# p times v in plain float32 with p summed beside it, and inputs laid out by the host, in a pooled attention with a feed-forward part

## The chip, the cores and the metric

The kernel runs on one core of a Trainium2 chip. The metric is device microseconds from start to end of one execution. Five engines have their own instruction streams, in order: TensorE (PE; its weight loads are listed apart as PEld), VectorE (DVE), ScalarE (ACT), GpSimd (POOL) and SyncE (SP), which here only issues DMAs.

## The reference

```
q, k, v: (8, 8, 1152, 64) float32; w_in (512, 2048), w_out (2048, 512)
q_pool = mean of neighbouring pairs of queries           # 576 queries of a head
scores = q_pool @ k.T / 8;  scores -= max over the keys
p = exp(scores);  p /= sum(p) + 1e-9
x = (p @ v), heads side by side                          # (4608, 512)
h = x @ w_in;  out = (h - tanh(h)) @ w_out               # (4608, 512)
```

The weights come as float64, which the kernel turns into float32 itself, from integer words.

## The kernel before, in words

Most products run on operands of type float32r (F32R), a float32 with a short mantissa. Every float32 is split into hi = f32r(x) and lo = f32r(x - hi), and a product of two of them is made of three: hi\*hi, hi\*lo and lo\*hi.

**Attention.** Heads are taken in 32 pairs (two heads fill 128 feature rows). A pair has `U` = 36 score units: two halves of the queries (288 each, `HQ`), three groups of three key tiles in each half, two heads, three key tiles. One `score_unit` is two products into a PSUM tile `ps_s` (`t1`: hi\*lo + lo\*hi by 128 contraction rows; `t2`: hi\*hi and minus the maximum by 66 rows) and an exponential on ScalarE, into `p_f`. Keys are on the partitions, queries run along the free axis.

*p times v* (`split_p`, `pv_slot`). ScalarE rounds three key tiles of exponentials to `p_h`; GpSimd (two in three) or VectorE (one in three) subtracts to get `p_l` in bfloat16. A 128-column operand `v_w` holds hi and lo of a head's v and a column of ones, so that one float32r product per key tile, head and half gives p_h times both parts of v and the sum of p. What is left (p_l times hi of v, p_l times one, p_h times the left-out column) are six bfloat16 products for each key tile, 32 or 64 columns wide, which are placed side by side on the array (`tile_position`). `v_part` prepares `v_w` on GpSimd.

*Maximum* (`max_part`, `max_rows`). For each pair, 27 products of 384 keys into `ps_m` (three buffers) and a VectorE `tensor_reduce` of each. Twenty-four of them contract over 64 rows only (one head), the three others over 128 rows with a block operand `bd`. `max_rows` takes the results through DRAM (`m_dram`) to two rows of `t2`.

*Preparation.* q and k are loaded with the tokens on the partitions; VectorE adds neighbouring queries (`query_sums`), TensorE transposes them (`transposes`), ScalarE and VectorE take hi and lo out of PSUM, and ten DMAs for a pair bring these to where the products need them (`operands`).

*Weights* (`w_block`). 64 blocks of 128x256 float64 words, each some eight VectorE operations and two of GpSimd, spread between the score units.

**Order.** In the attention part every engine keeps the order of the program (`InOrder`). The program goes through the 1152 units; a table (`units`, `rows`, `parts`) says how many units before its first score each step of a pair's preparation is issued, and `add(u, ...)` puts a task beside unit u. So an instruction that waits holds up everything behind it on its engine. DMAs are all issued by SP, in that same order.

**Feed-forward.** Ten chunks of columns: eight of 512 tokens and two of 256. For each there are 16 steps `fc`: `hidden` makes 12 products of 512 columns (hi and lo of x and w_in, `ps_h`), four ScalarE functions, seven VectorE operations and one of GpSimd give h - tanh(h) (the polynomial is used where u = h\*h is below a threshold, `copy_predicated` by a mask `g_m` takes the other value), then ScalarE and GpSimd split it (`g_hi`, `g_lo`). Two steps later (`LAG`) `second` makes 12 products with w_out. `load_x` brings the next chunk's x: for each of four feature tiles, DMAs (`fetch`), then an addition of the lo part on VectorE (L119) and three GpSimd operations (`work`, L120 to L122). Its staging tiles are single (`xt`), so a fetch follows the work before it. In this part a scheduler sets the order.

Of the kernel before, what the change touches and what calls it, by code (L numbers as in the profile page):

```python
# [10 lines left out]
BF16 = mybir.dt.bfloat16  # L11
# [7 lines left out]
# h - tanh(h) = PL * h * u * (u - P0) * ((u + A1)^2 + P1) * ((u + A2)^2 + P2), u = h^2,  # L19
# to float32 precision where |h| < T_POLY; h - tanh(h) itself cancels there  # L20
# [7 lines left out]
class InOrder:  # L28
    """An engine whose instructions keep the order they are written in."""
# [15 lines left out]
def kernel(  # L45
# [33 lines left out]
    pc = const.tile([P, 2], F32, name="pc")  # L79
    nc.vector.memset(pc[:, 0:1], A1)  # L80
    nc.vector.memset(pc[:, 1:2], A2)
    keep = const.tile([P, 1], F32, name="keep")      # 0 where x's lo rows hold the sums
    nc.vector.tensor_tensor(keep, ident[:, 63:64], ident[:, 64:65], op=ALU.add)
    nc.vector.tensor_scalar(keep, keep, -1.0, 1.0, op0=ALU.mult, op1=ALU.add)
# [3 lines left out]
    x_dram = dram.tile([NP, 2, P, NTOK], F32, name="x_dram")  # L88
# [5 lines left out]
    def load_x(tiles, sp, dve, pool, t0, n):  # L94
        """Columns of x, divided by the sums of their softmax, in two parts; in steps."""
# [4 lines left out]
        def fetch(hp):  # L100
            x = xt.tile([P, 512], F32, name="x_f")
            r = xt.tile([P, 512], F32, name="x_r")
            y = xt.tile([P, 512], F32, name="x_g")
            t[hp] = x, y, r
            rows = x_dram[hp].rearrange("h (u p) t -> (h u) p t", u=2)
            sp.dma_start(x[:, 0:n], rows[0:4:3, :, t0:t0 + n])
            sp.dma_start(y[:, 0:n], rows[1:3, :, t0:t0 + n])
# [9 lines left out]
        def work(hp):  # L117
            x, y, r = t[hp]
            dve.scalar_tensor_tensor(x[:, 0:n], y[:, 0:n], keep, x[:, 0:n], op0=ALU.mult, op1=ALU.add)  # L119
            pool.tensor_tensor(x[:, 0:n], x[:, 0:n], r[:, 0:n], op=ALU.mult)  # L120
            pool.tensor_scalar(x_h[:, hp, 0:n], x[:, 0:n], 1.0, 0.0, op0=ALU.mult, op1=ALU.add)  # L121
            pool.tensor_tensor(x_l[:, hp, 0:n], x[:, 0:n], x_h[:, hp, 0:n].bitcast(F32), op=ALU.subtract)  # L122
# [16 lines left out]
    with ExitStack() as actx:  # L139
        # what is free before the end comes last  # L140
# [15 lines left out]
        U = 4 * KT                  # score units of a pair: (half, three key tiles, head, key tile)  # L156
# [4 lines left out]
        tt = [[o.tile([P, 2, KQ], F32R, name=f"t{j}_{i}") for j in (1, 2)] for i, o in enumerate((op0, op))]  # L161
# [15 lines left out]
        nc.gpsimd.memset(one, 0.0)
# [509 lines left out]
```

## Time and profile before

| | |
|---|---|
| median of 3 runs | 2471.56 us (2467.0 to 2481.7) |
| the profiled execution: span | 2467.1 us; the lowest timed run has 2467.0 |
| first score product | at 27.5 us |
| attention ends, feed-forward begins | at 1493 us |
| PE, DVE, ACT, POOL busy over the span | 93%, 78%, 53%, 50% |
| mean granted TensorE clock | 0.88 |

A busy PE includes the time that a matmul's results take to come out, so it is not a PE at its peak; how far apart two products start says more. "L38" (L37 in the changed kernel) stands for all instructions of the attention part, since the helper class records them; they are told apart by the names of their tiles (`out<-in`). An idle time is put down to what ended it.

### The profile page before, as it was taken

How to read it: one execution, taken by the hardware profiler on the slowest of the kernel's cores; microseconds unless marked ns; L12 is line 12 of the kernel's file. 1: busy time of each engine (PE TensorE's matmuls, PEld its weight loads, DVE VectorE, ACT ScalarE, POOL GpSimd, SP SyncE). 2: the span in 40 equal slices, each digit the busy share in tenths (PEclk: the TensorE clock that was granted, in tenths of full speed). 3: DMA queues.
4: the chain of work that ended last, by engine and by line, in shares of the span. 5: the costliest groups of instructions: out<-in, count | busy, mean ns of one | idle time of the engine just before them, and what ended most of it. 6: DMA issues, size and time to landing. Idle time of an engine off the chain costs nothing. (4 is left out here: it accounts for less than half of the span.)

```text
span 2467.1 us, 34314 instructions
## 1 busy us (share of the span) xinstructions
PE 2289.9 (93%) x11921; PEld 1617.4 (66%) x11921; DVE 1926.3 (78%) x3119; ACT 1307.6 (53%) x2663; POOL 1241.7 (50%) x1022
## 2 busy tenths in 40 slices
PE   8999999999999999999999989779798897989988
PEld 5666666666666666666666667557676676767777
DVE  5687887977885868777867978678778786877988
ACT  2555665655664655655645665334444453444545
POOL 3455555555563545555645644554454544444443
PEclk9988887978895878978966979889999999999999
DMA  7355474564654744644644656120110202011010
GB/s 173 91 138 151 109 170 124 140 158 104 153 146 100 170 123 108 164 126 122 181 104 109 142 165 250 53 72 20 52 44 26 59 10 69 15 44 39 5 33 18
DMA packets 202180, 251.67 MB, mean 102 GB/s; under 512 B 92688, under 2 KB 131232, under 8 KB 202008
## 3 DMA queue, kind: packets, MB, share of 16 engines
q1 hardware_dynamic: 202008, 249.49, 38.6%
q8 instruction: 94, 1.54, 0.3%
q14 instruction: 78, 0.64, 0.1%
HBM read 118.93 MB, written 45.56 MB: 67 GB/s over the span
## 5 line engine op out<-in xcount | busy, mean ns | idle before, releaser
L38 POOL TENSOR_TENSOR p_l<-p_f,p_h 128x864 bf16<-128x864 f32 x256 | 531.2, 2078 | 655.9 <-ACT p_h L38 484.5
L38 ACT ACTIVATE p_f<-ps_s 128x288 f32<-128x288 f32 x1152 | 463.1, 412 | 573.0 <-PE ps_s L38 564.2
L38 DVE TENSOR_REDUCE mx<-ps_m 128x1 f32<-128x384 f32 x864 | 453.3, 550 | 295.7 <-PE ps_m L38 290.8
L38 PE MATMUL ps_s<-t 128*128 128x288 f32 (+1 forms) x2319 | 644.3, 368 | 9.1 <-DMA t<-m_dram 8.5
L38 PEld LDWEIGHTS ps_s<-t 128*128 128x128 f32 (+1 forms) x2319 | 429.9, 226 | 114.0 <-issue 23.8
L602 PE MATMUL ps_o<-wo,g_hi 128*128 128x512 f32 x1008 | 295.3, 416 | 70.7 <-ACT g_hi L594 70.7
L38 ACT ACTIVATE p_h<-p_f 128x864 fp32r<-128x864 f32 x384 | 353.0, 919 | 0.0
L575 PE MATMUL ps_h<-x,wi 128*128 128x512 f32 (+1 forms) x1440 | 334.9, 376 | 0.0
L595 POOL TENSOR_TENSOR g_lo<-g_s,g_hi 128x512 fp32r<-128x512 f32 (+1 forms) x160 | 202.3, 1265 | 258.1 <-ACT g_hi L594 186.9
L38 PE MATMUL ps_m<-x 64*128 64x384 f32 x768 | 304.5, 505 | 21.9 <-DVE mx L38 20.6
L38 PE MATMUL ps_o<-p_h,v_w 128*128 128x288 f32 x1152 | 312.9, 369 | 0.0
L575 PEld LDWEIGHTS ps_h<-x,wi 128*128 128x128 f32 x1440 | 262.6, 193 | 54.9
L602 PEld LDWEIGHTS ps_o<-wo,g_hi 128*128 128x128 f32 x1008 | 197.7, 200 | 125.0 <-ACT g_hi L594 83.5
L594 ACT ACTIVATE g_hi<-g_s 128x512 fp32r<-128x512 f32 (+1 forms) x160 | 94.2, 589 | 331.5 <-DVE g_s L593 326.8
L38 PEld LDWEIGHTS ps_o<-p_h,v_w 128*128 128x128 f32 x1152 | 219.6, 231 | 49.0 <-issue 48.5
L38 PEld LDWEIGHTS ps_m<-x 64*128 64x128 f32 x768 | 128.8, 211 | 143.3 <-issue 75.3
L38 PE MATMUL ps_o<-p_l,v_w 128*64 128x288 bf16 x1152 | 198.4, 341 | 0.0
L38 PE MATMUL ps_o<-p_h,v_x 128*32 128x288 bf16 x1152 | 190.9, 328 | 0.0
L38 PE MATMUL ps_o<-p_l,one 128*32 128x288 bf16 x1152 | 188.6, 323 | 0.1
L602 PE MATMUL ps_o<-wo,g_lo 128*128 128x512 f32 x504 | 165.5, 409 | 17.9 <-POOL g_lo L595 17.7
L38 DVE TENSOR_TENSOR p_l<-p_f,p_h 128x864 bf16<-128x864 f32 x128 | 170.3, 1331 | 3.1 <-ACT p_h L38 3.0
L38 DVE TENSOR_SCALAR w<-w 128x256 int32<-128x256 int32 (+1 forms) x192 | 165.9, 864 | 0.2
(82 smaller groups left out, 3171.3 us busy)
## 6 DMA issues: line engine op xcount, KB each, us to landing
t<-x SPq DMA_DIRECT2D x64, 432.0 KB
k_n<-in_k_dram SPq DMA_DIRECT2D x64, 288.0 KB
t<-kq_l SPq DMA_DIRECT2D x64, 288.0 KB
t<-x SPq DMA_DIRECT2D x64, 288.0 KB
v_n<-in_v_dram SPq DMA_DIRECT2D x32, 576.0 KB
x_dram<-o_s SPq DMA_DIRECT2D x32, 576.0 KB
q_n<-in_q_dram SPq DMA_DIRECT2D x32, 512.0 KB
t<-kq_l SPq DMA_DIRECT2D x64, 144.0 KB
```

The lines of the kernel that those rows point to most:

```text
L38: ins = self.tc.keep_in_program_order(f(*args, **kwargs))
L575: nc.tensor.matmul(h, wi[fc][:, w, c], x[:, c, 0:n], start=(j == 0), stop=(j == len(mm) - 1))
L594: nc.scalar.activation(g_h, s1, AF.Copy)
L595: nc.gpsimd.tensor_tensor(g_l, s1, g_h.bitcast(F32), op=ALU.subtract)
L602: nc.tensor.matmul(po[j], g[:, ts], wo[fc][:, w], start=(fc == 0 and i == 0), stop=(fc == NF - 1 and i == 2))
```

## The change

- **p times v.** `split_p`, `pv_slot` and `v_part` go. v is loaded by the host's layout and used as it is: for each key tile, half and head one product of plain float32 operands (`F32`, not `F32R`), v (64 columns) against the exponentials; the first head on array columns 0 to 63, the second on 64 to 127 (`pv`). All six of a group come in one burst.
- **Sums of p.** `z_part` adds the three key tiles of a group: GpSimd with two additions (groups 0 and 2 of a half), VectorE with one `tensor_reduce` over a strided view (group 1). For each half `z_sums` adds over the partitions with six plain float32 products by a block of ones, 32 columns wide, into `ps_z`. They go to DRAM by themselves (`z_dram`).
- **Layouts.** The host orders q, k and v so that the features are on the partitions; transposes go. The query sum is one addition of 128x576, on GpSimd (on VectorE for the first two pairs); hi and lo are taken from SBUF in two pieces. `kq_l` now has one buffer instead of two.
- **Maximum.** All 27 products contract over 128 rows, by a block operand of 128x1152 (`bd`) for each parity, that four DMAs of `max_queries` fill. `ps_m` has two buffers instead of three, `ps_s` four instead of three.
- **Weights.** 32 blocks of 128x512 instead of 64 of 128x256. The first 15 units' extra product goes.
- **Feed-forward.** L119 goes, and so does one of the two big DMAs of a fetch. The mask is made by ScalarE (Relu of u minus the threshold, read as integers). GpSimd's `s2` goes; its constant is added in a VectorE operation. VectorE has six operations instead of seven. The first chunk's `work` is on GpSimd instead of VectorE, and later. Output rows are contiguous.

The diff, cut to its core:

```diff
-            sp.dma_start(x[:, 0:n], rows[0:4:3, :, t0:t0 + n])
-            sp.dma_start(y[:, 0:n], rows[1:3, :, t0:t0 + n])
+            sp.dma_start(x[:, 0:n], x_dram[hp, :, t0:t0 + n])
...
-            dve.scalar_tensor_tensor(x[:, 0:n], y[:, 0:n], keep, x[:, 0:n], op0=ALU.mult, op1=ALU.add)
...
-        ps_m = actx.enter_context(tc.tile_pool(name="ps_m", bufs=3, space=PSUM))
-        ps_s = actx.enter_context(tc.tile_pool(name="ps_s", bufs=3, space=PSUM))
+        ps_m = actx.enter_context(tc.tile_pool(name="ps_m", bufs=2, space=PSUM))
+        ps_s = actx.enter_context(tc.tile_pool(name="ps_s", bufs=4, space=PSUM))
...
+        def max_queries(pi):
+            w = pairs[pi]
+            for h in range(2):
+                r = slice(h * 64, h * 64 + 64)
+                raw_copy(bd[w.i][r, h * 512:(h + 1) * 512], w.hi[r, 0:512])
+                raw_copy(bd[w.i][r, 8 * P + h * 64:8 * P + (h + 1) * 64], w.hi[r, 512:SQ])
...
-            pe.matmul(ps[:, 0:CH], st, mv, start=True, stop=True)
+            pe.matmul(ps[:, 0:CH], bd[w.i][:, t * P:(t + 1) * P], w.hi[:, cs], start=True, stop=True)
...
+        def z_part(grp):
+            z = grp.z = zp.tile([P, 2, HQ], F32, name="z")
+            if grp.g == 1:
+                dve.tensor_reduce(z, grp.p.rearrange("p h j q -> p h q j"), axis=AX.X, op=ALU.add)
+            else:
+                pool.tensor_tensor(z, grp.p[:, :, 0], grp.p[:, :, 1], op=ALU.add)
+                pool.tensor_tensor(z, z, grp.p[:, :, 2], op=ALU.add)
+        def pv(u, grp):
...
+            for j in range(3):
+                kt = 3 * grp.g + j
+                for h in range(2):
+                    pe.matmul(hf.o[64 * h:64 * h + 64, 0:HQ], w.v[:, h, kt], grp.p[:, h, j], start=(kt == 0),
+                              stop=(kt == KT - 1), tile_position=(0, 64 * h))
...
+        def z_sums(u, w, hf):
+            ps = ps_o.tile([P, 512], F32, name="ps_z")
+            for g in range(3):
+                for h in range(2):
+                    r = 64 * (g % 2) + 32 * h
+                    pe.matmul(ps[r:r + 32, 0:HQ], ones, hf.zs[g][:, h], start=(g < 2), stop=(g > 0),
+                              tile_position=(0, r))
...
-            units = dict(load=-93, load_k=-76, query_sums=-82, transposes=-69, last_queries=-53, operands=-36, load_v=-33,
-                         v_part=-18)
+            units = dict(load=-82, query_sums=-68, hi_q=-66, hi_k=-65, max_queries=-64, lo_q=-62, lo_k=-61, operands=-34, load_v=-20)
...
-        nc.gpsimd.tensor_scalar(s2, s2, 1.0, P2, op0=ALU.mult, op1=ALU.add)
+        nc.scalar.activation(m, u, AF.Relu, bias=pc[:, 2:3])
...
-        nc.vector.scalar_tensor_tensor(s1, s1, P1, s2, op0=ALU.add, op1=ALU.mult)
-        nc.vector.tensor_tensor(s1, s1, w, op=ALU.mult)
-        nc.vector.tensor_scalar(m, u, T_POLY * T_POLY, None, op0=ALU.is_ge)
-        last = nc.vector.copy_predicated(s1, m, th).ins
+        nc.vector.scalar_tensor_tensor(w, s2, P2, w, op0=ALU.add, op1=ALU.mult)
+        nc.vector.scalar_tensor_tensor(s1, s1, P1, w, op0=ALU.add, op1=ALU.mult)
+        last = nc.vector.copy_predicated(s1, m.bitcast(I32), th).ins
```

Where instructions stand now. TensorE in the middle of the attention part, before: one key tile's bfloat16 products (v_x, one and v_w are their operands) between two score units and a product for the maximum (ps_m).

```order
L38 MATMUL ps_m_5271<-x_4595 128x384
L38 LDWEIGHTS v_x0_128
L38 MATMUL ps_o0_5226<-p_h_5073,v_x0_128 32x288
L38 LDWEIGHTS v_x0_128
L38 MATMUL ps_o1_5227<-p_h_5123,v_x0_128 32x288
L38 LDWEIGHTS one_130
L38 MATMUL ps_o0_5226<-p_l_5074,one_130 32x288
L38 LDWEIGHTS one_130
L38 MATMUL ps_o1_5227<-p_l_5124,one_130 32x288
L38 LDWEIGHTS v_w01_125
L38 MATMUL ps_o1_5227<-p_l_5124,v_w01_125 64x288
```

The same engine in the middle of the attention part now, where a group's p times v stands between score units.

```order
L37 MATMUL ps_s_10227<-t1_0_121 128x288
L37 MATMUL ps_s_10227<-t2_0_122 128x288
L37 MATMUL ps_o_10178<-p_f_10114,v_9850 64x288 x6
L37 MATMUL ps_s_10238<-t1_0_121 128x288
L37 MATMUL ps_s_10238<-t2_0_122 128x288
L37 MATMUL ps_m_10242<-x_10097,bd0_125 128x384
L37 MATMUL ps_s_10248<-t1_0_121 128x288
L37 MATMUL ps_s_10248<-t2_0_122 128x288
```

The column-tiled products, which came in three short visits for a group, now come in one of six. VectorE, before, in the middle of the attention part: reductions for the maximum between weight steps (w), lo parts (kq_l) and subtractions for p_l.

```order
L38 TENSOR_TENSOR p_l<-p_f,p_h 128x864
L38 TENSOR_SCALAR w_9629<-w_9628 128x256
L38 TENSOR_TENSOR kq_l<-ps_m,x 128x512
L38 SCALAR_TENSOR_TENSOR w_9630<-w_raw,w_9629 128x256
L38 TENSOR_REDUCE mx<-ps_m 128x1 x5
```

VectorE now, at a like place, with a lo part that waits for the DMAs out of the one `kq_l` buffer, and a reduction of p (z).

```order
L37 TENSOR_REDUCE mx<-ps_m 128x1 x5
L37 TENSOR_TENSOR kq_l<-kq,x 128x576
L37 TENSOR_REDUCE mx<-ps_m 128x1
L37 TENSOR_TENSOR kq_l<-kq,x 128x1152
L37 TENSOR_SCALAR w_hl<-w_6599 128x512
L37 TENSOR_REDUCE mx<-ps_m 128x1
L37 TENSOR_REDUCE z<-p_f 128x576
```

The maxima that follow a lo part or a z stand behind it; p_l is gone from this engine.

More of the change, by code (lines that the diff above doesn't have):

```diff
@@ L78 @@
     nc.vector.tensor_copy(ident_r, ident)
-    pc = const.tile([P, 2], F32, name="pc")
+    pc = const.tile([P, 3], F32, name="pc")
     nc.vector.memset(pc[:, 0:1], A1)
     nc.vector.memset(pc[:, 1:2], A2)
[L82 to L88, printed above, removed]
+    nc.vector.memset(pc[:, 2:3], -T_POLY * T_POLY)
+    ones = const.tile([P, 32], F32, name="ones")
+    nc.vector.memset(ones, 1.0)
+    x_dram = dram.tile([NP, P, NTOK], F32, name="x_dram")
+    z_dram = dram.tile([B, 2, 2, NP, SQ], F32, name="z_dram")
     r_dram = dram.tile([B, 2, NP, SQ], F32, name="r_dram")
@@ L102, in fetch @@
             r = xt.tile([P, 512], F32, name="x_r")
-            y = xt.tile([P, 512], F32, name="x_g")
-            t[hp] = x, y, r
-            rows = x_dram[hp].rearrange("h (u p) t -> (h u) p t", u=2)
-            sp.dma_start(x[:, 0:n], rows[0:4:3, :, t0:t0 + n])
-            sp.dma_start(y[:, 0:n], rows[1:3, :, t0:t0 + n])
+            t[hp] = x, r
+            sp.dma_start(x[:, 0:n], x_dram[hp, :, t0:t0 + n])
             c = t0
@@ L231, in query_sums, with hi_part @@
             w.mx = sm.tile([P, 9, 3], F32, name="mx")
             w.hi = x_tile(0)[:, 0:KQ]
-            w.lo = tr.tile([P, KQ], F32R, name="kq_l")
-        def transposes(u, pi, g):
+            w.lo = ld.tile([P, KQ], F32R, name="kq_l")
+        def hi_part(pi, c0, c1):
             w = pairs[pi]
-            blocks = [(w.q_s[:, t], P) for t in range(4)] if g == 0 else []
-            blocks += [(w.q_s[0:64, 4], 64)] if g == 1 else []
-            blocks += [(w.k_n[:, c], P) for c in ((), range(0, 3), range(3, 7), range(7, KT))[g]]
-            ps = ps_m.tile([P, 512], F32, name="ps_m")
-            n = 0
-            for src, m in blocks:
-                pe.transpose(ps[:, n:n + m], src.rearrange("p h d -> p (h d)"), ident[0:m, 0:m])
-                n += m
-            c0 = (0, 512, SQ + 3 * P, SQ + 7 * P)[g]
-            cs = slice(c0, c0 + n)
-            add(u + 1, lambda: act.activation(w.hi[:, cs], ps[:, 0:n], AF.Copy), at=first)
-            add(u + 3, lambda: dve.tensor_tensor(w.lo[:, cs], ps[:, 0:n], w.hi[:, cs].bitcast(F32), op=ALU.subtract))
@@ L376, in pv_out @@
-        def pv_out(u, w, o, half):
-            if half == 0:
-                w.o_s = sm.tile([P, 2, SQ], F32, name="o_s", bufs=1)
-            for h in range(2):
-                act.activation(w.o_s[:, h, half * HQ:(half + 1) * HQ], o[h][:, 0:HQ], AF.Copy)
-            if half == 1:
-                c0 = w.b * SQ
-                add(u + 2, lambda: sp.dma_start(x_dram[w.hp, :, :, c0:c0 + SQ].rearrange("h p t -> p h t"), w.o_s))
+            pass
+        def z_part(grp):
[5 more added lines that the diff above has]
+                pool.tensor_tensor(z, z, grp.p[:, :, 2], op=ALU.add)
@@ new lines, in pv @@
+        def pv(u, grp):
+            w, hf = grp.w, grp.half
+            if grp.g == 0:
+                hf.o = ps_o.tile([P, 512], F32, name="ps_o")
+                hf.zs = []
+            for j in range(3):
[3 more added lines that the diff above has]
+                              stop=(kt == KT - 1), tile_position=(0, 64 * h))
+            hf.zs.append(grp.z)
+            if grp.g == 2:
+                add(u + 1, o_out, w, hf, at=first)
+                add(u + G - 1, z_sums, u + G - 1, w, hf)
@@ new lines, in z_out, with store @@
+        def z_out(u, w, hf, ps):
+            act.activation(w.z_s[:, hf.n * HQ:(hf.n + 1) * HQ], ps[:, 0:HQ], AF.Copy)
+            if hf.n == 1:
+                def store():
+                    sp.dma_start(x_dram[w.hp, :, w.b * SQ:(w.b + 1) * SQ], w.o_s)
+                    for r in range(4):
+                        sp.dma_start(z_dram[w.b, r // 2, r % 2, w.hp:w.hp + 1], w.z_s[32 * r:32 * r + 1])
+                add(u + 2, store)
+                if w.hp == NP - 1:
+                    add(u + 6, lambda: tot.append((w.b, sums(w.b))))
+                    if w.b < B - 1:
+                        add(u + 12, lambda: reciprocals(dve, *tot[0]))
+                        add(u + 15, lambda: spread(sp, *tot.pop(0)))
@@ L386, in sums @@
         def sums(b):
             n = NP * 2 * SQ // P
[L389 to L392 removed]
+            t = rec.tile([P, 2, n], F32, name="rec")
+            for r in range(2):
+                for h in range(2):
+                    sp.dma_start(t[h * 64:h * 64 + 64, r], z_dram[b, r, h].rearrange("a (x n) -> (a x) n", n=n))
@@ L449 @@
             for r in range(f // P, (f + WB) // P):
-                for c in range(0, DM, WB):
-                    blocks.append((1, r, c))
+                blocks.append((1, r, 0))
         for i, blk in enumerate(blocks):
-            u = U + 18 * i - 3 * max(i - 47, 0)
+            u = U // 2 + 34 * i
             add(u, w_block, u, *blk)
@@ L511 @@
             add(u + units["load_v"], load_v, pi)
-            for h in range(2):
-                add(u + units["v_part"] + 18 * h, v_part, pi, h)
             for x, ta, tb in rows:
```

267 lines of the change are left out of this document (88 added, 179 removed).

## The prediction

> **What bounds the kernel now.** I began with the clock, since the page's mean of 0.88 hides two states. Two stretches of the attention part, all engines (us, then busy time and count of PE, PEld, DVE, ACT, POOL, granted clock, DMA share, GB/s):
>
> ```profile
> 280.00:350.00 70.00, 67.97 (x465) 44.34 (x465) 62.80 (x106) 48.22 (x106) 42.07 (x31) 1.00 0.49 132
> 750.00:802.00 52.00, 52.00 (x219) 33.17 (x219) 25.81 (x56) 22.56 (x48) 17.77 (x15) 0.50 0.36 93
> ```
>
> The same two stretches for the score tile `ps_s` alone (PE, PEld, ACT); ACT's count is the number of score units:
>
> ```profile
> 280.00:350.00 70.00, 31.48 (x132) 20.11 (x132) 26.06 (x67) 1.00 0.49 132
> 750.00:802.00 52.00, 22.91 (x60) 15.70 (x61) 12.30 (x30) 0.50 0.36 93
> ```
>
> At full clock a unit takes 70/67 = 1.045 us, a pair of 36 units 37.6 us; at half clock 52/30 = 1.73 us, a pair 62.4. At full clock VectorE is busy for 62.80/70 = 0.90 and TensorE for 0.97: both are nearly used up. At half clock TensorE alone is.
>
> The whole part has its ends in the rows of the first scores and of the first feed-forward product:
>
> ```profile
> L38 PE MATMUL ps_s<-t x2319: 288/300/611, 27.5 to 1482.5; 66*128 66x288 f32 x190, 128*128 128x288 f32 x4
> ```
>
> ```profile
> 1493.03 6.64 PE L575 MATMUL ps_h<-x,t 128*128 128x512 f32 x28
> ```
>
> So it takes 1493 - 27.5 = 1465 us, 45.8 for each of 32 pairs: a mixture of the two states. The feed-forward part has the other 974 us.
>
> What TensorE pays for a product is how far the starts are apart (start, us, form, count), first at full clock, then at half:
>
> ```profile
> 821.14 0.55 PE L38 MATMUL ps_m<-ident,k_n 128*128 128x128 f32 x3
> 821.45 0.51 PE L38 MATMUL ps_o<-p_h,v_w 128*128 128x288 f32 x2
> 821.79 0.43 PE L38 MATMUL ps_s<-t 128*128 128x288 f32 x2
> 822.07 0.34 PE L38 MATMUL ps_m<-x,bd 128*128 128x384 f32 x1
> 822.24 0.43 PE L38 MATMUL ps_o<-p_h,v_w 128*128 128x288 f32 x2
> 822.51 0.43 PE L38 MATMUL ps_s<-t 128*128 128x288 f32 x2
> ...
> 823.40 0.31 PE L38 MATMUL ps_o<-p_h,v_x 128*32 128x288 bf16 x2
> 823.40 0.30 PE L38 MATMUL ps_o<-p_l,one 128*32 128x288 bf16 x2
> 823.63 0.32 PE L38 MATMUL ps_o<-p_l,v_w 128*64 128x288 bf16 x2
> 823.88 0.54 PE L38 MATMUL ps_s<-t 128*128 128x288 f32 x2
> ```
>
> ```profile
> 761.14 0.92 PE L38 MATMUL ps_o<-p_h,v_w 128*128 128x288 f32 x3
> 761.86 0.68 PE L38 MATMUL ps_s<-t 128*128 128x288 f32 x2
> ```
>
> Two float32r products of 288 columns take 0.27 us (822.24 to 822.51), so 0.135 each; 384 columns take 0.17. Four narrow products start together and cost 0.23, not 0.135: going from one tiling of the array to another costs some 0.1. At half clock three products take 0.72, 0.24 each.
>
> **The change part by part: TensorE in the attention.** For a pair: scores 72 x 0.135 = 9.7. Maximum, now 27 products on 128 rows, 27 x 0.17 = 4.6, without the changes of tiling around the 64-row ones. Transposes go. p times v: 18 key tiles (9, two halves), two heads side by side. No row shows a plain float32 product. Its price lies between one float32r pass (0.135) and four (0.54). The nearest row is the transposes of float32 tiles: three of 128 columns in 0.31 us, 0.23 for 288. I take 0.54, above it: the kernel's own splitting shows that the array's operand holds half of a float32, and a whole product of two split numbers is four part products (the kernel before keeps three). 18 x 0.54 = 9.7. Sums of p: two visits of four and two tiles, 4 x 0.54 = 2.2. Eight visits to column tiles, two changes each: 1.6. Transposed maxima: 0.2, an estimate. Together 28.0 us at full clock; at the transposes' price it would be 21.2. At half clock it is (9.7 + 9.7 + 2.2) x 0.24/0.135 + 4.6 x 2 + 1.8 = 49.4.
>
> The Trainium skill ("FP8 and Floating Point Precision", TensorE Precision Notes) has true float32 at four passes; the sum by it is the 28.0. No run here shows it yet.
>
> **VectorE in the attention** decides, I think. Its rows (busy us, mean ns):
>
> ```profile
> L38 DVE TENSOR_REDUCE mx<-ps_m 128x1 f32<-128x384 f32 x864 | 453.3, 550 | 295.7 <-PE ps_m L38 290.8
> L38 DVE TENSOR_TENSOR kq_l<-ps_m,x 128x512 fp32r<-128x512 f32 x64 | 43.7, 683 | 18.9 <-ACT x L38 18.9
> L38 DVE CAST m<-nm 128x10 fp32r<-128x10 f32 x30 | 13.7, 458 | 1.0
> L38 DVE TENSOR_SCALAR w<-w 128x256 int32<-128x256 int32 (+1 forms) x192 | 165.9, 864 | 0.2
> L38 DVE TENSOR_SCALAR w<-w_raw 128x256 int32<-128x256 int32 x128 | 93.2, 728 | 0.0
> L38 DVE SCALAR_TENSOR_TENSOR w<-w_raw,w 128x256 f32<-128x256 uint16 x64 | 62.0, 969 | 0.2
> L38 DVE SCALAR_TENSOR_TENSOR w<-w,w 128x256 int32<-128x256 int32 x64 | 34.4, 538 | 0.8
> L38 DVE TENSOR_SCALAR w_hl<-w 128x256 fp32r<-128x256 f32 x64 | 23.3, 364 | 4.4 <-POOL w L38 4.4
> ```
>
> and, for what 512 columns cost when nothing is in the way (min/median/max ns):
>
> ```profile
> L38 DVE TENSOR_TENSOR x_f<-x_f,x_r x4: 691/692/694, 1433.8 to 1473.6; 128x512 f32<-128x512 f32 x4
> L38 DVE TENSOR_SCALAR x<-x_f x4: 426/428/428, 1434.5 to 1474.3; 128x512 fp32r<-128x512 f32 x4
> ```
>
> For a pair: 27 maxima x 0.550 = 14.85. Two sums of p, 1728 elements read each: at the maximum's rate (550/384 = 1.43 ns) 2.47 each, 4.95; contiguous reads at 692/512 would make it 4.7; the stride is weighed below. lo parts, 1728 columns at 683/512: 2.3. Rows of the maximum: the rounding 0.46 and three smaller ones, 1.0 (estimate). Weights: now (165.9 + 93.2 + 62.0 + 34.4 + 23.3)/32 = 11.8; blocks twice as wide with nothing in the way would take 6 x 0.428 + 2 x 0.692 = 3.95 each, 4.2 for a pair at 34 units a block. A scalar step took 864 ns on average where 428 is the price of twice its width, so it waits for something, most likely GpSimd's use of the same memory. GpSimd has less to do now, in shorter pieces; I take the middle, 8.0. The 128 subtractions for p_l and the small copies go. Sum 31.1 (27.3 to 34.9). At VectorE's share of 0.90 that is 34.5 us a pair, against TensorE's 28.0; before it was 37.6 at full clock and 62.4 at half.
>
> The clock: I estimate the array's work as rows x columns in use. Before, a pair has 44,000 full columns (scores 15,700, p_h 10,400, maximum 5,800, narrow products 10,400, transposes 1,700). In 62.4 us at half clock that is 0.29 of what 2.4 GHz allows (288 columns in 0.12 us), and there the clock stays down; in 37.6 it is 0.49. Afterwards it is 50,000 with four passes: 0.42 at half clock, 0.61 in 34.5 us. So I expect full clock nearly throughout.
>
> Waits that are added. `kq_l` has one buffer: the lo part of the next pair waits for the operand DMAs, issued 8 units (7.7 us) before; behind it in VectorE's queue are the maxima, and TensorE waits for those with two `ps_m` buffers.
>
> ```profile
> q1 hardware_dynamic: 202008, 249.49, 38.6%
> ```
>
> 249.49 MB in 0.386 of 2467 us is 262 GB/s; the last `kq_l` copy ends 1.73 MB into the ten copies, 6.6 us: just in time. I take 0, and up to 3 us a pair (+96 us). ScalarE's hi part waits for GpSimd's sum of queries, issued two units before; behind it are the exponentials, covered by four `ps_s` buffers. SP also issues four small copies into `bd` and four stores of sums; nothing late is put behind them, 0 to 1 us a pair. ScalarE loses the p_h copies, GpSimd p_l; both had room and have more. Two GpSimd additions for each of four groups, at about the row of 512 columns below, 1.6 us, take 13 of 34.5 us.
>
> **The feed-forward part.** A step costs TensorE 5.54 us once it runs (two starts of `hidden`), and a chunk's first half takes longer than its second (8 of 16 steps in each):
>
> ```profile
> 1512.36 2.96 PE L575 MATMUL ps_h<-x,wi 128*128 128x512 f32 x12
> ...
> 1517.90 2.96 PE L575 MATMUL ps_h<-x,wi 128*128 128x512 f32 x12
> ```
>
> ```profile
> 1820.00:1880.00 60.00, 4.69 (x8) 0.94 0.23 70
> 1880.00:1927.00 47.00, 4.77 (x8) 1.00 0.01 2
> ```
>
> 107 us against 16 x 5.54 = 89: 18 lost for each of eight loads (the halves together as one), 144 in all. Why is seen in the waits (us in total, times, longest) and in the steps of the load:
>
> ```profile
> DVE x_f L119 <- DMA x_f<-x_dram: 110.3, 33, 5.5
> ```
>
> ```profile
> L119 DVE SCALAR_TENSOR_TENSOR x_f<-x_g,keep,x_f x36: 483/751/753, 1542.5 to 2372.7; 128x512 f32<-128x512 f32 x28, 128x256 f32<-128x256 f32 x8
> L120 POOL TENSOR_TENSOR x_f<-x_f,x_r x36: 735/1474/1672, 1543.4 to 2373.2; 128x512 f32<-128x512 f32 x28, 128x256 f32<-128x256 f32 x8
> L121 POOL TENSOR_SCALAR x<-x_f x36: 404/936/1127, 1545.1 to 2374.6; 128x512 fp32r<-128x512 f32 x28, 128x256 fp32r<-128x256 f32 x8
> L122 POOL TENSOR_TENSOR x<-x_f,x x36: 725/1590/1799, 1546.2 to 2375.4; 128x512 fp32r<-128x512 f32 x28, 128x256 fp32r<-128x256 f32 x8
> ```
>
> ```profile
> L586 POOL TENSOR_SCALAR g_s<-g_s 128x512 f32<-128x512 f32 x128 | 109.3, 854 | 64.4 <-ACT g_s L585 56.5 <-POOL g_lo L595 0.2
> ```
>
> VectorE stood still for the DMA with the polynomial behind it. That wait now falls to GpSimd alone, with `g_lo` behind it. Gone from the path of each feature tile are L119 (0.75), L586 (0.85) and a DMA's issue (0.3, estimate): 1.9 x 4 x 8 = 61. I take 60, between 0 (the wait on GpSimd costs the same) and 144. The mask on ScalarE and one VectorE operation less cost nothing while TensorE's 5.54 us hides them; the mask's single buffer makes ScalarE wait for the step before, which is over by then. The first chunk's load, moved late onto GpSimd, is 4 x 4.0 = 16 us, partly after the last product: +10 (0 to 20). The start stays at 27.5 (its maxima and DMAs are the same), +/-10.
>
> **Sum**: 27.5 + 32 x 34.5 + 10 + (974 - 60) = 2055.5 for the span. The profiled span, 2467.1, is the lowest run; the median is 4.5 above. 2060.
>
> **Rivals.**
> - *VectorE's strided sum is dear.* The sum of p reads words 1152 bytes apart. The row of `w_raw` reads every second word and shows no price for 8 bytes of step; no row has a longer one. If it took twice as long: 4.95/0.90 = 5.5 a pair, 176 us: 2236. The Trainium skill ("SBUF — State Buffer", Specifications) wants two hits in each line of 16 bytes for full rate, which speaks for this rival. Chance 0.12.
> - *The two column tiles don't run beside each other in plain float32.* The bfloat16 ones do (two starts at 823.40). Otherwise p times v costs 9.7 more and the sums 4.3: 42.0 a pair on TensorE, 1344: 2300. Chance 0.12.
> - *The clock stays at half: slower.* If three of the four passes don't count as work, a pair has 32,000 columns: 0.27 at half clock, under the 0.29 at which it stays down before. Then 49.4 x 32 = 1581: 2537. It turns slower than before from 0.86 of the pairs at half clock on ((47.3 - 34.5)/(49.4 - 34.5)). Against it: at full clock even that is 0.39. Chance 0.09. The Trainium skill ("TensorE: Matmul & The Clock Gate", Part 1) lets the clock fall when the array is idle; by that this rival could not be. The row 750 to 802, busy 52.00 of 52.00 us at 0.50, differs, and the measurement decides.
> - Several small waits that eat up the gain, 0.05.
>
> **How the numbers follow.** Forecast 0.62, with its own range of 1940 (TensorE's 28.0 at a share of 0.90 sets the pair, 1951, and the start or the feed-forward part gives 10 more) to 2200 (34.9 on VectorE, 38.8 a pair; the lo parts' wait would make 2156). The range 1940 to 2300 takes in the strided sum and the edge of the serial tiles. 0.5% (12 us) is about what a measurement can tell. Faster 0.86 (three cases), same 0.03, slower 0.11 (the clock, some of the small waits).
>
> **What would show it.** Clock near 1.0 in the attention part; units 0.96 us apart; VectorE at 0.9 there, TensorE with idle time ended by `mx`; pairs of `pv` products starting together, 0.54 apart; z on VectorE near 2.5 us; feed-forward near 914 us. Wrong: a clock of 0.5 for long, z over 4 us, pv products one after the other, VectorE waiting for DMAs at `kq_l`.

## The result, and the profile after

The changed kernel takes 2037.6 us (median of 4 runs, 2035.0 to 2046.2), the kernel before beside it 2476.6: a ratio of 0.832, 95% interval 0.822 to 0.842. The prediction said 2060, in a range from 1940 to 2300. The total came out; two of its terms did not, and they made up for each other. Ratios and intervals, here and below, leave out executions that are longer as a whole than the others of the same kernel (one of e1's four took 3349.5 us); the medians hold all. The profiled execution's span is 2043.1 us; it is the longest of the four.

The windows of the changed kernel, all engines, with the columns of the prediction's first rows: the attention part, an undisturbed stretch of it, a disturbed one, the feed-forward part.

```profile
31.00:1200.00 1169.00, 1026.59 (x6217) 678.98 (x6219) 819.54 (x1373) 544.11 (x1373) 488.30 (x351) 0.94 0.63 166
677.80:752.00 74.20, 67.83 (x442) 45.34 (x440) 57.97 (x96) 39.75 (x99) 32.31 (x24) 1.00 0.68 178
316.20:326.00 9.80, 5.32 (x20) 3.20 (x21) 6.51 (x12) 1.23 (x3) 2.80 (x2) 0.50 0.38 117
1212.00:2043.00 831.00, 805.16 (x3640) 656.89 (x3640) 727.95 (x962) 534.87 (x996) 348.03 (x273) 0.99 0.15 50
```

The second of them for the score tile alone (PE, PEld, ACT), 81 units in 74.2 us:

```profile
677.80:752.00 74.20, 34.39 (x162) 26.72 (x162) 31.14 (x81) 1.00 0.68 178
```

A unit is 0.916 us at full clock, where it was 1.045. VectorE is busy for 0.78 of this stretch and for 0.70 of the whole part, far from the 0.90 on which the forecast stood. TensorE has 0.91. The part's ends, from the rows of the score tile and a timeline (the last row is the first function of the feed-forward part):

```profile
L37 PE MATMUL ps_s<-t x2304: 288/296/610, 22.6 to 1199.2; 128*128 128x288 f32 x192
L37 ACT ACTIVATE p_f<-ps_s x1152: 391/411/455, 31.2 to 1199.7; 128x288 f32<-128x288 f32 x192
```

```profile
1227.02 0.60 ACT L520 ACTIVATE g_u<-ps_h 128x512 f32<-128x512 f32 x1 [17.00 <-PE ps_h L514]
```

The same end in the kernel before:

```profile
1484.38 4.85 PE L575 MATMUL ps_h<-x,t 128*128 128x512 f32 x20
1487.50 0.60 ACT L582 ACTIVATE g_u<-ps_h 128x512 f32<-128x512 f32 x1 [3.35 <-PE ps_h L575]
```

So 1493.03, where the prediction let the feed-forward part begin, is not its first product; 20 of them stand ahead of it. That moves 5.5 us from one part to the other and leaves the sum as it is. With the same cuts in both kernels (first score, end of the last exponential, first `g_u`, end) and the time at half clock added up between the exponentials:

| us | start | attention | to the first `g_u` | feed-forward | half clock in attention |
|---|---|---|---|---|---|
| before | 27.5 | 1455.7 | 4.3 | 979.6 | 481 |
| after | 22.6 | 1177.5 | 26.9 | 816.1 | 150 |

So of 424 us the attention gave 278, the feed-forward part 163.5, the start 5, and 22.6 were lost in between.

**p times v** on TensorE, in one burst (start, us, form, records):

```profile
703.69 1.68 PE L37 MATMUL ps_o<-p_f,v 128*64 128x288 f32 x12
705.29 0.54 PE L37 MATMUL ps_s<-t 128*128 128x288 f32 x2
705.67 0.34 PE L37 MATMUL ps_m<-x,bd 128*128 128x384 f32 x1
705.85 0.70 PE L37 MATMUL ps_s<-t 128*128 128x288 f32 x4
```

A plain float32 product is two records; six products make twelve, and the next start comes 1.60 us after the first: 0.53 for each key tile with both heads. The prediction had 0.54. Twelve records one after the other, at 0.133 each, would take as long as six pairs side by side; e8 below tells the two apart. (By the Trainium skill, "FP8 and Floating Point Precision", TensorE Precision Notes, it is four passes: 4 x 0.135 = 0.54 agrees.) A maximum product on 128 rows holds the array for 0.18 us (705.67 to 705.85).

**VectorE's groups** (busy us, mean ns, idle before and what ended it):

```profile
L37 DVE TENSOR_REDUCE mx<-ps_m 128x1 f32<-128x384 f32 x864 | 455.5, 552 | 206.9 <-PE ps_m L37 196.8
L37 DVE TENSOR_REDUCE z<-p_f 128x576 f32<-128x1728 f32 x64 | 136.3, 2130 | 61.5 <-ACT p_f L37 52.0 <-POOL x L37 9.5
L37 DVE TENSOR_SCALAR w<-w 128x512 int32<-128x512 int32 (+1 forms) x96 | 59.2, 617 | 0.2
L37 DVE TENSOR_SCALAR w<-w_raw 128x512 int32<-128x512 int32 x64 | 43.6, 681 | 30.5 <-DMA w_raw<-in_moe_w_out_dram 17.2 <-DMA w_raw<-in_moe_w_in_dram 13.4
```

Nothing is dear there. The strided sum takes 1.23 ns an element, a maximum 1.44. But a good part of the shorter instruction is fixed: 34 reductions of 6 elements (`nm<-mx`) take 154 ns each. Without that part it is 1.15 against 1.05, so by this estimate the stride costs about a tenth, and not a doubling. What is new are waits (engine, tile, what ended them: us in all, times, longest), in three answers for PE, PEld and DVE:

```profile
PE ps_m L37 <- DVE mx L37: 140.1, 146, 8.1
...
PEld ps_m L37 <- DVE mx L37: 213.8, 315, 8.3
```

```profile
DVE mx L37 <- PE ps_m L37: 196.8, 171, 4.4
DVE z L37 <- ACT p_f L37: 52.0, 32, 9.6
...
DVE kq_l L37 <- DMA t<-kq_l: 31.7, 10, 7.8
...
DVE w L37 <- DMA w_raw<-in_moe_w_out_dram: 17.2, 8, 5.4
DVE w L37 <- DMA w_raw<-in_moe_w_in_dram: 13.4, 6, 5.9
```

TensorE and VectorE wait for each other at `ps_m`, and VectorE for DMAs. One such stall, on SP, VectorE and TensorE:

```profile
305.78 3.17 SPq L37 DMA_DIRECT2D t<-x  x3
...
309.72 2.03 SPq L37 DMA_DIRECT2D w_raw<-in_moe_w_out_dram  x1
```

```profile
317.70 0.43 DVE L37 TENSOR_SCALAR w<-w_raw 128x512 int32<-128x512 int32 x1 [5.45 <-DMA w_raw<-in_moe_w_out_dram]
```

```profile
320.69 0.69 PE L37 MATMUL ps_m<-x,bd 128*128 128x384 f32 x1 [7.27 <-DVE mx L37]
321.17 1.64 PE L37 MATMUL ps_s<-t 128*128 128x288 f32 x6
322.74 3.15 PE L37 MATMUL ps_o<-p_f,v 128*64 128x288 f32 x12
```

The load of a block of weights is issued at 309.72, behind operand copies in SP's queue. Its first step, 8 units behind it in the program instead of 12, comes before it has landed: it stands still for 5.45 us with the maxima behind it; TensorE stops for 7.27, and the window 316 to 326 ran at half clock, where the burst of `p_f,v` takes 3.15 us.

**The feed-forward part**, one chunk, 8 of its 16 steps in each row (ACT at L520, granted clock, DMA share, GB/s):

```profile
1494.90:1540.50 45.60, 4.72 (x8) 1.00 0.22 64
1540.50:1583.90 43.40, 4.77 (x8) 1.00 0.03 6
```

The first half, with the next chunk's load in it, took 60 us and now takes 45.6, hardly more than the second (43.4).

### The profile page after: what moved, and what is told of

It reads as the page before. It is cut to its first block, busy times and chain, and to the rows that moved or that the text cites. A ratio compares the mean times of both kernels' runs of the same rounds, so it can differ in the third digit from the quotient of the medians.

```text
span 2043.1 us, 28793 instructions
## 1 busy us (share of the span) xinstructions
PE 1851.3 (91%) x9922; PEld 1346.1 (66%) x9922; DVE 1561.9 (76%) x2365; ACT 1083.6 (53%) x2375; POOL 850.8 (42%) x640
## 4 chain that ended last, share of the span: by engine, by line
PE 49%; DVE 21%; DMA 13%; POOL 7%; issue 4%; SPq 3%; ACT 3%; POOLq 0%; DVEq 0%; ACTq 0%
PE ps_o L539 10%; PE ps_h L514 10%; PE ps_s L37 10%; PE ps_o L37 9%; PE ps_m L37 7%; DVE mx L37 6%; DVE z L37 6%; DMA x_f<-x_dram 3%; DMA t<-kq_l 3%; SPq L37 3%; DVE w L37 3%; POOL x L120 2%; POOL x_f L118 2%; DVE kq_l L37 2%; PE ps_z L37 2%
## 5 line engine op out<-in xcount | busy, mean ns | idle before, releaser
L37 PE MATMUL ps_s<-t 128*128 128x288 f32 (+1 forms) x2304 | 503.2, 319 | 4.2 <-DMA t<-m_dram 4.2
L37 PE MATMUL ps_m<-x,bd 128*128 128x384 f32 x864 | 340.3, 396 | 150.0 <-DVE mx L37 135.9
L37 POOL TENSOR_TENSOR z<-p_f 128x576 f32<-128x576 f32 x128 | 182.3, 1424 | 487.6 <-ACT p_f L37 487.4
L37 PE MATMUL ps_o<-p_f,v 128*64 128x288 f32 x2304 | 359.4, 452 | 0.0
L37 PEld LDWEIGHTS ps_m<-x,bd 128*128 128x128 f32 x864 | 171.4, 199 | 216.9 <-DVE mx L37 201.2
L37 PEld LDWEIGHTS ps_o<-p_f,v 128*64 128x64 f32 x2304 | 160.5, 148 | 128.8 <-issue 57.0
L37 POOL TENSOR_TENSOR z<-z,p_f 128x576 f32<-128x576 f32 x128 | 184.4, 1440 | 12.4 <-ACT p_f L37 2.8
L37 DVE TENSOR_REDUCE z<-p_f 128x576 f32<-128x1728 f32 x64 | 136.3, 2130 | 61.5 <-ACT p_f L37 52.0
L527 DVE SCALAR_TENSOR_TENSOR g_w<-g_w,g_u 128x512 f32<-128x512 f32 (+1 forms) x160 | 173.5, 1084 | 0.0
L520 ACT ACTIVATE g_u<-ps_h 128x512 f32<-128x512 f32 (+1 forms) x160 | 87.7, 548 | 125.0 <-PE ps_h L514 124.5
L530 DVE COPY_PREDICATED g_s<-g_m,g_t 128x512 f32<-128x512 int32 (+1 forms) x160 | 135.5, 847 | 14.7 <-DVE g_s L529 0.5
```

The lines of the kernel that those rows point to most:

```text
L37: ins = self.tc.keep_in_program_order(f(*args, **kwargs))
L520: nc.scalar.activation(u, h, AF.Square)
L527: nc.vector.scalar_tensor_tensor(w, w, PL, u, op0=ALU.mult, op1=ALU.mult)
L530: last = nc.vector.copy_predicated(s1, m.bitcast(I32), th).ins
```

## The experiments

The medians stand beside the kernel before on the same chip (2452 to 2473 us there); the parts come from one profiled execution each. Where a part of a kernel is all but unedited, it shows the spread: the attention of the kernel before took 1425 to 1456 us in three executions (before, e7, e12), that of the changed kernel 1163 to 1178 in three (after, e4, e13). The changed kernel's own trace, 1177.5, is at the upper end, and so is before's, 1455.7. The parts:

| us | median | attention | to `g_u` | feed-forward | half clock | ratio to before, 95% |
|---|---|---|---|---|---|---|
| e1, weights loaded earlier | 2001.7 | 1133.6 | 27.7 | 816.1 | 120 | 0.805 to 0.822 |
| e5, two `kq_l` | 2005.8 | 1136.2 | 27.8 | 815.9 | 102 | 0.809 to 0.823 |
| e6, three `ps_m` | 1967.7 | 1105.0 | 25.7 | 815.3 | 133 | 0.793 to 0.807 |
| e9, sums on GpSimd | 2004.2 | 1137.3 | 27.6 | 816.4 | 140 | 0.806 to 0.824 |
| e2, maximum on 64 rows | 2209.1 | 1332.8 | 26.9 | 814.2 | 328 | 0.893 to 0.914 |
| e3, before, maximum on 128 rows | 2297.9 | 1285.6 | 4.3 | 975.3 | 188 | 0.934 to 0.949 |
| e4, a load step on VectorE | 2035.5 | 1172.4 | 27.2 | 809.4 | 167 | 0.827 to 0.840 |
| e7, before, new `hidden` | 2461.5 | 1432.8 | 4.3 | 975.5 | 420 | 0.999 to 1.014 |
| e12, before, load split | 2371.3 | 1425.1 | 4.3 | 869.4 | 403 | see there |
| e13, load on two engines | 2218.8 | 1162.8 | 46.7 | 982.6 | 130 | 0.904 to 0.922 |
| e8, half of p times v | 2035.7 | 1161.7 | 26.5 | 815.7 | 123 | 0.826 to 0.841 |
| e10, all together | 1866.0 | 1015.9 | 6.5 | 825.8 | 61 | 0.761 to 0.774 |

**What sets the attention part.** Theory A: VectorE's stalls for late DMAs. B: VectorE's own work, as the prediction had it. C: the coupling at `ps_m`. In e1 each block's load is issued 6 units earlier, and the steps, counted from it, come 6 units later, so that they stay where they were:

```diff
-            for i, op in ((8, begin),
+            for i, op in ((14, begin),
...
-            u = U // 2 + 34 * i
+            u = U // 2 - 6 + 34 * i
```

> The changed kernel, with each block of weights loaded 14 units before its first VectorE step instead of 8; the steps stay where they are. Theory A (in the attention part VectorE stands still for late DMAs, and the clock falls behind it): the waits for w_raw, 31 us in all, go, and with them part of the half-clock stretches; 30 to 60 us less, about 2000 us. Theory B (VectorE's own work sets the pair, as the prediction had it): 10 us less at most. Theory C (the two ps_m buffers couple TensorE and VectorE too tightly, whatever else happens): 10 us less at most.

```diff
-            w.lo = ld.tile([P, KQ], F32R, name="kq_l")
+            w.lo = ld.tile([P, KQ], F32R, name="kq_l", bufs=2)
```

> The changed kernel with two buffers for kq_l instead of one. Theory A: VectorE's wait for the copies of kq_l (31.7 us in 10 waits) goes, with the clock's falls behind it; 25 to 50 us less. Theory B and theory C: 10 us less at most.

```diff
-        ps_m = actx.enter_context(tc.tile_pool(name="ps_m", bufs=2, space=PSUM))
-        ps_s = actx.enter_context(tc.tile_pool(name="ps_s", bufs=4, space=PSUM))
+        ps_m = actx.enter_context(tc.tile_pool(name="ps_m", bufs=3, space=PSUM))
+        ps_s = actx.enter_context(tc.tile_pool(name="ps_s", bufs=3, space=PSUM))
```

> The changed kernel with three ps_m and three ps_s buffers, as before, instead of two and four. Theory C: TensorE's waits for ps_m (140 us with its weight loads' 214 beside them) fall by at least half, 30 to 60 us less. Theory A: 0 to 20 less, a stall of VectorE reaches TensorE one product later. Theory B: no change, within 10 us. If the fourth ps_s buffer is what covers ScalarE, it gets slower, by 10 to 40.

```diff
-            if grp.g == 1:
+            if False:
```

> The changed kernel with all sums of p on GpSimd, so that VectorE loses two sums of 2.13 us a pair. Theory B (VectorE's work at its highest share, 0.78 as measured, sets the pair): 4.3/0.78 = 5.5 us a pair, 175 us less. Theory A and theory C: VectorE has room, 0 to 40 us less; if GpSimd's longer work slows VectorE at their common memory, 0 to 30 us more.

e1 took 44 us out of the attention, e5 41, e6 72.5, e9 40, against the one trace of the changed kernel. By the medians of whole runs it is 36, 32, 70 and 33. In e1 VectorE's waits for `w_raw` are down from 30.6 us to 0.3 and those for `kq_l` (first row below) from 31.7 to 10.8; in e5 those for `kq_l`'s copies are gone and those for `w_raw` stay (the other two):

```profile
DVE kq_l L37 <- DMA t<-kq_l: 10.8, 6, 6.6
```

```profile
DVE w L37 <- DMA w_raw<-in_moe_w_out_dram: 24.2, 7, 6.8
DVE w L37 <- DMA w_raw<-in_moe_w_in_dram: 19.6, 6, 7.1
```

In e6 the weight loads' waits for `mx` (213.8 before the edit) fall by 40%, less than the half that was expected, while the time falls by more:

```profile
PEld ps_m L37 <- DVE mx L37: 127.2, 139, 7.0
```

Theories A and C both hold, and B falls. In e9 VectorE's busy time in the attention part goes from 819.5 to this row's 713.0 us, but the part shrinks by 40 us and not by 175; 52 us of VectorE's waits, those before the sums, went in the same edit.

```profile
31.00:1160.00 1129.00, 1012.30 (x6219) 676.28 (x6221) 713.01 (x1308) 542.02 (x1372) 689.99 (x478) 0.94 0.65 172
```

**The maximum on 128 rows.** e2 takes it out of the changed kernel, as below; in e3 the two `bd` and `max_queries` are put into the kernel before, and all 27 products read `bd` there.

```diff
-            pe.matmul(ps[:, 0:CH], bd[w.i][:, t * P:(t + 1) * P], w.hi[:, cs], start=True, stop=True)
+            if t < 8:
+                h, j = divmod(t, 4)
+                r = slice(h * 64, h * 64 + 64)
+                st, mv = w.hi[r, j * P:(j + 1) * P], w.hi[r, cs]
+            else:
+                st, mv = bd[w.i][:, t * P:(t + 1) * P], w.hi[:, cs]
+            pe.matmul(ps[:, 0:CH], st, mv, start=True, stop=True)
```

> The changed kernel with 24 of a pair's 27 maximum products on 64 rows again, as before. Theory T (what the array's tiling changes cost: some 0.1 us for each way, on TensorE's path): up to 24 x 0.2 = 4.8 us a pair, 60 to 150 us more in all, and more where the clock falls for longer. Theory R (TensorE has room in the attention part, as its waits for VectorE show): 0 to 20 us more.

> The kernel before with only the maximum changed: all 27 products on 128 rows by two block operands that four copies for each pair fill (p_f has six buffers instead of seven, to make room). Theory T with the clock following the array's work: full-clock units 0.95 us instead of 1.09 and fewer at half clock, 150 to 350 us less. Theory R (VectorE's share of 0.90 set the unit before): within 40 us of before.

Taken out of the changed kernel it costs 155 us of attention; put into the one before it saves 170. With the spread of the unedited parts this is 155 to 170 and 140 to 170. Theory T holds at both ends, R falls. Starts in e2:

```profile
509.07 0.44 PE L37 MATMUL ps_m<-x 64*128 64x384 f32 x1
509.44 0.53 PE L37 MATMUL ps_s<-t 128*128 128x288 f32 x2
509.90 0.44 PE L37 MATMUL ps_m<-x 64*128 64x384 f32 x1
```

A 64-row product holds the array for 0.37 us where the 128-row one held it for 0.18, and the two score products behind it take 0.46 where two cost 0.27 without a change of tiling: 0.38 for each of 24, more than the 0.2 expected. (The Trainium skill, "TensorEngine Tiling (Array Packing)", Key Properties, says that a change of tiling mode drains the array; these rows agree.) Two windows of e2, one after the other:

```profile
501.30:535.40 34.10, 34.00 (x182) 19.25 (x178) 26.16 (x40) 16.05 (x40) 12.37 (x10) 1.00 0.67 179
535.50:549.10 13.60, 13.60 (x48) 7.20 (x47) 3.68 (x7) 4.10 (x11) 4.03 (x3) 0.50 0.53 167
```

TensorE is busy throughout, without a stall, and the clock still falls to half. (A busy TensorE includes the time in which results come out, so this does not show that the array was full.) Of 42 such falls in e2's attention part, 31 come behind less than 0.3 us without a product in the 6.8 us before; in the changed kernel all 27 come behind 1.4 to 4.4 us. e2 spends 328 us at half clock, for 153 units that would take 149 at the 0.971 us that lie between two of its exponentials at full clock, 179 lost. The changed kernel's 150 us held 61 units, 56 us at 0.913: 94 lost, stalls in them included. By this estimate the difference, 85 us, is over half of e2's 155; the longer products, some of which fill TensorE's waits for VectorE, are the rest.

**Does the clock follow the array's work?** e8 leaves out 7 of 9 products of p times v for the second head.

```diff
-                for h in range(2):
+                for h in range(2 if kt in (0, KT - 1) else 1):
```

> The changed kernel with 7 of 9 products of p times v left out for the second head of each pair (its x is therefore not the reference's); those of the first head stay, so that each burst holds four of six products or three. If the two column tiles run beside each other in plain float32, as the trace shows, and the clock follows the work that the array does: full-clock units as long as before, 0.90 to 0.92 us, but the array has some 15% less work, so more of the attention part at half clock, 250 us instead of 150, and the kernel 30 to 120 us slower although it does less. If they run beside each other and the clock doesn't depend on that work: no change, within 15 us. If the products of the two heads paid for each other: some 7 us a pair less, 1820 to 1900 in all.

```profile
700.71 1.67 PE L37 MATMUL ps_o<-p_f,v 128*64 128x288 f32 x6
```

Six records take what twelve took: the second head's products were free, so the column tiles run side by side. The clock did not fall more often (123 us at half). That the clock follows rows times columns in use finds no support here, though by the prediction's own sums the 16% less that this leaves, 0.51 instead of 0.61, would still lie above the 0.49 that held full clock before. What it follows stays open.

**Where the feed-forward part's 164 us came from.** e4 puts the load's first multiplication on VectorE (`first`); e7 puts the new `hidden` into the kernel before.

```diff
-            pool.tensor_tensor(x[:, 0:n], x[:, 0:n], r[:, 0:n], op=ALU.mult)
+            first.tensor_tensor(x[:, 0:n], x[:, 0:n], r[:, 0:n], op=ALU.mult)
```

> The changed kernel with the first multiplication of each later load of x (x by 1/sum) on VectorE instead of GpSimd, so that VectorE waits again for the load's DMA; the number of operations stays. Theory D (the feed-forward part gained because VectorE no longer waits for DMAs with the polynomial behind it): 60 to 130 of the 164 us come back. Theory O (it gained because hidden has one VectorE and one GpSimd operation less): within 20 us, either way.

> The kernel before with only the edits of hidden: mask by ScalarE, no GpSimd operation ahead of the polynomial, six VectorE operations (some constants lie in another pool, to make room). Theory O: 80 to 160 us less. Theory D: 0 to 50 less, since L119 still waits for its DMA on VectorE.

Neither moved it: 809 against 816, and 975.5 against 979.6. Theory O falls. D falls as it was put: VectorE again stood behind the load in e4, but had little to wait for, 20 us against 110:

```profile
DVE x_f L118 <- DMA x_f<-x_dram: 13.1, 20, 1.6
...
DVE x_f L118 <- DMA x_r<-r_dram: 7.0, 5, 2.1
```

So the copies themselves had become quicker. The DMA view of the kernel before, from the issue of one `x_f` copy (1830.14) until it has landed, in 40 slices of 0.2 us:

```profile
DMA  6544324001000111011111111111111111111000
GB/s 109 130 78 135 130 88 93 10 10 31 31 31 31 52 31 52 31 41 41 62 41 62 41 62 41 62 41 52 52 52 52 41 62 41 62 41 62 0 0 0
```

After other traffic the copy runs alone, at a tenth of the engines and some 50 GB/s: 256 KB in 5 to 6 us. In the trace its 128 packets of 2 KB go two at a time, 84 ns each (median). Its source is `rows[0:4:3]`, two blocks of 64 rows with a gap. (The Trainium skill, "DMA: Bandwidth & Descriptors", Why a DMA increments its semaphore by 16 and not by 1, lets the outermost dimension of the two sides decide how many of the 16 engines share a copy; with 2 there it is two. The trace, two packets at a time, agrees.) The changed kernel's single copy is of 128 rows that follow each other. Theory F says that this is the gain.

```diff
-            sp.dma_start(x[:, 0:n], rows[0:4:3, :, t0:t0 + n])
+            for i in range(2):
+                sp.dma_start(x[i * 64:i * 64 + 64, 0:n], rows[3 * i, :, t0:t0 + n])
-            sp.dma_start(y[:, 0:n], rows[1:3, :, t0:t0 + n])
+            for i in range(2):
+                sp.dma_start(y[i * 64:i * 64 + 64, 0:n], rows[1 + i, :, t0:t0 + n])
```

> The kernel before with each of the two big copies of a fetch of x issued as two, of 64 whole rows each, same bytes. Theory F (in the kernel before these copies ran on 2 of the 16 DMA engines, since their source is two blocks of 64 rows: 256 KB at 49 GB/s, 5.3 us, and it is this length that VectorE and GpSimd wait for): copies of some 2.5 us, the feed-forward part 80 to 140 us shorter than its 980. Theory G (what counts is that there is a second copy and VectorE's addition L119 behind it, whatever their length): within 30 us.

```diff
-            sp.dma_start(x[:, 0:n], x_dram[hp, :, t0:t0 + n])
+            rows = x_dram[hp].rearrange("h (u p) t -> (h u) p t", u=2)
+            sp.dma_start(x[:, 0:n], rows[0:4:3, :, t0:t0 + n])
...
```

In e13 `x_dram` has room for two blocks of 128 rows again, and two stores of 64 rows fill it where there was one of 128.

> The changed kernel with x kept in DRAM as before, in two blocks of 64 rows that do not follow each other, so that its single copy for each feature tile goes through the same two DMA engines as before; nothing else of the load changes. Theory F: the feed-forward part gets 60 to 140 us longer than its 816, with waits of GpSimd for x_f. Theory G: within 20 us.

e12's feed-forward part is 110 us shorter than before's, with the same bytes, one more instruction for each copy, and L119 still there. e13's is 166.5 longer than the changed kernel's, as long as it ever was, and its load between the two parts costs 20 more. F holds, G falls. Whole runs of e12 lie between 2328 and 2406 us, those of before beside it between 2417 and 2474; they spread too far for an interval. The wait of VectorE at the addition that was L119 has sunk from 110.3 us to one of 0.2; in e13 GpSimd's wait at its first operation on x (here L119, L118 in the changed kernel), 44.9 there, has grown:

```profile
POOL x_f L119 <- DMA x_f<-x_dram: 238.1, 35, 8.6
```

What the slow copies cost TensorE, in before, e12 and e13 (all engines, the feed-forward part from the first `g_u` to the end):

```profile
1487.50:2467.10 979.60, 855.25 (x3675) 682.50 (x3673) 788.42 (x1158) 449.29 (x838) 459.13 (x428) 0.95 0.16 51
1456.80:2326.20 869.40, 814.69 (x3675) 652.19 (x3673) 789.44 (x1158) 449.37 (x838) 463.78 (x428) 1.00 0.19 57
1232.10:2214.60 982.50, 852.46 (x3615) 686.36 (x3613) 693.12 (x962) 530.81 (x996) 324.25 (x268) 0.93 0.11 40
```

TensorE is idle for 124 us in before, 55 in e12, 130 in e13, and 20 in the changed kernel, where the clock is 1.00 as well and TensorE busy for 796 us. So of the 163.5 us, 104 were stalls and 59 busy time. Some 4 of these 59 are the attention's last products, which in before run behind the first `g_u`; the rest fits the half clock, 104 us in before's part, 143 in e13's and 3 in e12's and in the changed kernel's. Stalls and clock both go with the copies. The 53 us between e12 and the changed kernel were not taken apart: one copy instead of two, L119 and the operations of `hidden` go together there, and e7 tried `hidden` only behind slow copies.

One detail of the expectation was wrong: only the copy of `x_f` ran on two engines. That of `x_g`, of rows that follow each other, reached over 300 GB/s (one of them in the kernel before, issued at 1838.84, in slices of 0.16 us from 1838.80):

```profile
DMA  0000005846798400012224232436464369987999
GB/s 0 0 0 0 0 0 128 128 90 192 307 358 333 154 0 0 0 51 90 90 90 134 90 109 83 102 96 71 51 128 167 115 192 250 243 218 192 230 205 205
```

**All together.** e10 has the edits of e1, e5, e6 and e9, and this:

```diff
-        add(end - 15, lambda: x0.extend(load_x(lambda: (x_tile(0), x_tile(0)), sp, pool, *chunks[0])))
+        add(end - 52, lambda: x0.extend(load_x(lambda: (x_tile(0), x_tile(0)), sp, pool, *chunks[0])))
...
-                add(end - 14 + 8 * j + 5 * i, lambda i=i, j=j: x0[2][j][i]())
+                add(end - 51 + 10 * j + 6 * i, lambda i=i, j=j: x0[2][j][i]())
```

> The changed kernel with four edits together, the earlier load of the weights, two buffers for kq_l, three ps_m buffers and all sums of p on GpSimd, and with the first chunk's load of x begun 52 units before the end instead of 15. If the stalls that they take away are separate: 1177 - 44 - 41 - 72 - 40 = 980 us of attention, 20 less behind it, about 1825 in all. If they are one stall seen at different places: about 1100 and 20 less, 1940. TensorE's own work by the prediction, 28.0 us a pair, allows 900 at the least.

1866.0 us, 0.767 of before (0.761 to 0.774), 172 us under the changed kernel's median. The four edits took 161.6 us out of the attention. Their single gains add up to 197 by the traces and to 171 by the medians, so the stalls are mostly separate; how much of them is shared can't be told from this. The step between the parts fell from 26.9 to 6.5 us, of which the feed-forward part gave 10 back. A window of e10, all engines, and its score tile:

```profile
480.50:685.00 204.50, 198.32 (x1358) 138.10 (x1354) 167.08 (x287) 117.74 (x297) 157.71 (x104) 1.00 0.80 210
```

```profile
480.50:685.00 204.50, 106.67 (x500) 82.05 (x500) 95.05 (x249) 1.00 0.80 210
```

0.821 us a unit, 29.6 a pair, TensorE busy for 0.97: here TensorE comes closest to setting the time, VectorE's waits are mostly for it (198.0 us at `ps_m` in the whole run), and the prediction's 28.0 for its work is nearly what is left.

## Why the prediction was right, and where it was wrong

- **TensorE's prices: right.** A pair of float32 products 0.53 (0.54 said), side by side (e8), 29.6 us a pair where nothing stops it (28.0 said for its work).
- **The saving by the maximum's tiling: right in kind, never priced by itself.** It is 140 to 170 of the attention's 278 us. The rest, with p times v and the layouts in it, was not taken apart.
- **"VectorE in the attention decides", at a share of 0.90: wrong.** Its work was mis-sized: 31.1 us a pair were said, and its instructions' own times add up to 27.3 (the weights 5.6 instead of 8.0, the sums 4.3 instead of 4.95), or to 819.5/32 = 25.6 where overlapping ones are counted once. Its share reached 0.70. The share of 0.90 came from the kernel before and was taken over as if it belonged to the engine; in a full-clock stretch of e3 it is 0.94 (70.42 of 75.10 us).
- **The added waits: taken at 0, wrong.** `kq_l` cost 41 us (0 to 96 was given). The two `ps_m` buffers were named as the way by which a stall reaches TensorE, but given no price: 72.5. The load of the weights, now 8 units ahead instead of 12, was not seen at all: 44. Together these and the sums' place make 162 us: a pair took 1177.5/32 = 36.8 us, and without them (e10) 1015.9/32 = 31.7. The 34.5 between the two came from too much work on VectorE and no waits. The rival of small waits had the mechanism, not the size.
- **The first chunk's load, +10: 22.6 measured** (26.9 - 4.3). The product waits for GpSimd until 1220.09:

```profile
1203.10 1.20 PE L514 MATMUL ps_h<-x,t 128*128 128x512 f32 x4
...
1220.09 10.24 PE L514 MATMUL ps_h<-x,t 128*128 128x512 f32 x36 [5.87 <-POOL x L37]
```

- **The feed-forward part, 60 us off: 163.5 measured**, above the 144 given as the most. The step that failed is the list of what goes from the path: it counted instructions, and left the copy of `x_f` at its old length. That copy's 5 us were in the trace (VectorE's longest wait was 5.5) and were taken for a wait that GpSimd would inherit.
- **The sum.** Attention and what lies behind it gained 255.6 us where 351 were forecast, the feed-forward part 163.5 where 60 were, the start 4.9. Two errors of about 100 us cancelled. That was luck, and 2060 against 2037.6 is no proof of the steps.
- **The rivals.** The strided sum took 2130 ns, where the forecast had 2470 and the rival twice that. (The Trainium skill, "SBUF — State Buffer", Specifications, wants two hits in each line of 16 bytes for full rate; at steps of 1152 bytes the rows show about the tenth worked out above, and the measurement decides.) The column tiles run together. The clock stays up: 0.96 over the span.

## What to carry to other kernels

An engine's share of busy time in one kernel is not its ceiling in the next: where engines run in order and wait for each other through two or three buffers, price each wait, and test with one more buffer. Price a copy by its own time in the DMA view, and look at its share of the engines: one that runs alone at a tenth of them may be slow by its shape, and here joining or splitting its rows was worth more than the instructions saved behind it. Check a good total by its terms.

## What the hardware showed that was not expected

- Copies of 256 KB whose source was two separate blocks of 64 rows ran at some 50 GB/s, one whose 128 rows follow each other at over 300; this alone was 110 to 166 us of the feed-forward part, most of it TensorE's stalls and the clock that fell with them.
- The clock fell to half while TensorE was busy for 13.60 of 13.60 us, in e2, where 64-row products stand among 128-row ones (328 us at half clock; before, with such products too: 481). With the maximum on 128 rows it was 188 (e3) and 150, and every fall there came behind at least 0.6 us of idle TensorE in the 6.8 us before. Why the clock falls in a busy stretch stays open.
- A 64-row product of 384 columns between 128-row ones held the array twice as long as a 128-row one (0.37 against 0.18 us), and slowed the two products behind it by 0.19.
